# The last V in the buffer of the last K but one, and the MLP's weights behind it

## The chip, the cores and the metric

The kernel runs on one core of a Trainium2 chip. A core has five engines, each with an instruction stream of its own: TensorE (PE in the profile; its weight loads are shown as PEld), VectorE (DVE), ScalarE (ACT), GpSimd (POOL) and SyncE (SP), which here only issues transfers. They wait for each other through semaphores. Each engine works its stream strictly in order, so an instruction that waits holds back all that is behind it. The metric is the device time of one execution in microseconds (us), the median over several runs.

## What is computed

One decoding step of a parallel block: attention over a cache, and beside it an MLP, both added to the input. There are 8 batches, 32 heads with a K and a V of their own each (no sharing), 4096 cached keys, 128 elements a head, a model width D of 640, and 1728 hidden units in the MLP. All tensors are bf16.

```python
def _A_ref(x, k_cache, v_cache, wq, wo):
    q = (x @ wq).reshape(B, 1, 32, 128).transpose(0, 2, 1, 3)
    scores = einsum("bhqd,bhkd->bhqk", q, k_cache) * 128 ** -0.5
    p = softmax(scores)
    o = einsum("bhqk,bhkd->bhqd", p, v_cache)
    return o.transpose(0, 2, 1, 3).reshape(B, 1, 4096) @ wo

def _B_ref(x, w1, b1, w2, b2):
    h = gelu(layernorm(x) @ w1 + b1)
    return h @ w2 + b2

xn = layernorm(x)
return x + _A_ref(xn, k_cache, v_cache, wq, wo) + _B_ref(xn, w1, b1, w2, b2)
```

The two caches hold 256 MiB each and are read once. Everything else together is some 15 MB.

## The kernel before

**Turns.** The work on the caches is cut into NQ = 32 turns; turn i takes one batch and HS = 8 heads. For each turn one K tile and one V tile are loaded whole: 128 partitions with 256 keys of 128 elements each, 64 KB on a partition, 8 MB in all. A partition holds 256 consecutive keys of one head; 16 partitions make a head.

**Buffers.** `S_sb` holds three such slots: KA for the K of even turns, KB for the K of odd turns, VS for every V. All else that is large borrows from them. wq lies in VS before the first V comes. The buffers of the MLP (w1, w2, the hidden values, the widened tail of w1, w2's tail `w2b`) and the selection matrices `selW` and `sel` lie in KA, the rows of wo in KB (woW, woL).

**Scores.** Of the 256 keys on a partition, TensorE takes 80: `pe_T` transposes them in groups of 8, ScalarE copies the result out of PSUM (`act_T`), and `pe_QK` multiplies with the query. VectorE takes the other 176 in three chunks (`dve_chunk`): a product with the query spread over the partitions, a fold that adds one half of each row to the other, and a reduce of what is left. The fold is the second TENSOR_TENSOR of a chunk in the profile. `dve_sel` brings TensorE's scores beside VectorE's, `dve_max` finds the maxima, and `act_exp` computes the exps of 8 heads, with their row sums.

**Product with V.** `pe_RS` adds up the row sums over the partitions and `pe_PV` multiplies the probabilities with V, 256 matmuls in one accumulation. Both of turn i stand in TensorE's stream behind the scores of turn i + 1. `act_O` (ScalarE) copies the result out and `o_norm` (GpSimd; in the last turn VectorE) divides by the sums.

**Behind the turns.** The result has heads and batches in an order that the product with wo can't use, so it is sorted by products with selection matrices: `pe_selw` and `pe_sel` on TensorE, `dve_foldw` and `dve_fold` on VectorE. `fin_wl` and `fin_wn` multiply with wo, whose rows come in six transfers (`load_wl`, `load_wn`), the last ones small. The MLP is `pe_mlp1`, `act_gelu` and `pe_mlp2`; `widen` on GpSimd copies the tail of w1 into a wider layout for it. All of this adds to one sum in PSUM, `ACC_ps`; `fin_store` copies it out and stores it in two halves.

**The order of the work** is written out by hand. `at(position, function)` files each step under a number, Q = 100 for a turn; the steps are sorted by it and called, and each appends its instructions to the list of its engine. Waits are set from the tickets of the steps (`tk`), and a wait that an earlier one of the same engine covers is left out. Then `_replay` writes each list out. For TensorE, VectorE and ScalarE the turns are written as a loop: `_steps` looks for the instructions whose waits grow from turn to turn, and they take their number from the loop's register.

**SyncE's queue** carries all large transfers, in the order of the stream: K i before V i. A K waits until the K before it in its slot has been used (`kt`, `km`, later `exp`), a V until the product with the last V is done (`pv`). The MLP's weights (`load_mlp`, `load_w2b`) wait for the end of K 30's use in KA, so they stand between V 30 and V 31. V 31 waits for the product with V 30, as every V does for the one before. wo waits for the end of K 31's use in KB. V 30 is loaded in two parts (V_CUT: 192 and 64 of the 256 keys), the second with a semaphore of its own (`ld_vl`), for which TensorE waits inside its 256 matmuls. So that the same wait can stand in every turn, the semaphore is raised by 1 at the beginning, by a memset of `consts_pool`, and the number waited for is 1 before turn 30 and 17 from then on.

**TensorE's loop** has 32 turns. The first half of a turn (spread query and scores) is skipped in the last one, by a branch, the second half (sums and product with V) is done in all 32. Behind it stand two stretches under a branch of their own which are done only in turn 31: the MLP's first layer, and the sorting of what is finished by then with the MLP's second layer (`pe_mlp2` at position NQ·Q + 4.6). So in time the MLP's layers come ahead of the sums and product of the last turn. What is left, the product with wo and the sorting of the last turn's result (`pe_sel(3, 1)`), is straight code behind the loop.

The branches of the loop, cut to what decides:

```python
with e.If_lt(reg, n):
    ...                                 # first half
for call in second[0]: ...              # second half
for part in (first[-1][:cut - head[-1]], first[-1][cut - head[-1]:]):
    with e.If_eq(reg, n - 1):
        _replay(e, part)                # MLP; sorting and second layer
```

Of the kernel before, what the change touches and what calls it, by code (L numbers as in the profile page):

```python
# [14 lines left out]
P = 128  # L15
# [100 lines left out]
def _replay(e, calls):  # L116
    for call in calls:
        _emit(e, call)
# [43 lines left out]

def _replay_pe(e, calls, head, mid, end, cut, late):

    n = len(head)
    first = [calls[a:b] for a, b in zip(head, mid)]
    second = [calls[a:b] for a, b in zip(mid, head[1:] + [end])]
    g1, g2 = _steps(first[:-1]), _steps([[c for c in t if not _late(c, late)] for t in second])
    _replay(e, calls[:head[0]])
    with e.bass.Fori(1, n + 1, engines=OrderedEngineSet([e.engine])) as r:  # L170
        reg = e.to_reg(r)
        with e.If_lt(reg, n):
            for call, step in zip(first[0], g1):
                _emit(e, call, call[1][1] + (r - 1) * step if step else None, r)
        g = iter(g2)
        for call in second[0]:
            if _late(call, late):
                e.wait_ge(call[1][0], (r + 1 >> (n.bit_length() - 1)) * 16 + 1)
            else:
                step = next(g)  # L180
                _emit(e, call, call[1][1] + (r - 1) * step if step else None)
        for part in (first[-1][:cut - head[-1]], first[-1][cut - head[-1]:]):
            with e.If_eq(reg, n - 1):
                _replay(e, part)
    assert n & (n - 1) == 0
    _replay(e, calls[end:])


def _late(call, late):
    return call[0] == "wait_ge" and any(call[1][0] is x for x in late)  # L190


def bass_parallel_sum__gqa_block_cached__mixer_channel_mlp__decode_kernel(
# [13 lines left out]
    B, _, D = A_x.shape  # L207
# [31 lines left out]
    WN_CUT = (0, 5 * CT, 7 * CT, 7 * CT + CT // 2, HS * CT)  # L239
    V_CUT = (0, 192, 256)  # L240

# [18 lines left out]
    with ExitStack() as es:  # L260
# [19 lines left out]
        w2_sb = scratch(FB * D, P, KA).rearrange("p (c n) -> p c n", n=D)  # L280
        hT_sb = scratch((FB + FS) * B, P, KA).rearrange("p (c b) -> p c b", b=B)
        b1_sb = scratch(F, 1, KA)
        w1x_sb = scratch(DC * FS * FR, P, KA).rearrange("p (c s n) -> p c s n", c=DC, s=FS)
        b1x_sb = scratch(FS * FR, 1, KA).rearrange("p (c s n) -> p c s n", c=1, s=FS)
        w2b_sb = scratch(FS * D, FR, KA).rearrange("p (s n) -> p s n", s=FS)
        selW_sb = scratch(HW * P, P, KA).rearrange("p (c h r) -> p c h r", c=HW, h=HW)
        sel_sb = scratch(HS * P, P, KA).rearrange("p (c h r) -> p c h r", c=HS, h=HS)
        out_sb = scratch(D, B, KA)
        woW_sb = part(KB, 0, HW * D)
# [61 lines left out]
            _Dma(sem(n)) for n in ("ld_x", "ld_b1", "ld_b2", "ld_wq", "ld_w1", "ld_w2a", "ld_w2b", "st_a", "st_o"))  # L351
        ld_vl = [_Dma(sem(f"ld_vl{q}")) for q in range(1, len(V_CUT) - 1)]
        ld_wl = [_Dma(sem(f"ld_wl{q}")) for q in range(2)]
# [4 lines left out]
        def at(pos, fn, *a):  # L358
            prog.append((pos, len(prog), fn, a))
# [8 lines left out]
        def load_k(i):  # L368
# [7 lines left out]
            tk[("k", i)] = ld_s[s].sig(sp.dma_start(tile[s], cache_src(A_k_cache, i)))  # L376

        def load_mlp():
            sp.wait(tk[("kt", NQ - 2)], tk[("km", NQ - 2)])
            load("w1", ld_w1, w1_sb, B_w1.rearrange("(p c) f -> p c f", c=DC))  # L380
            load("w2a", ld_w2a, w2_sb, B_w2[0:FB * P, :].rearrange("(p c) n -> p c n", c=FB))

        def load_v(i):
            sp.wait(tk["qmm"] if i == 0 else tk[("pv", i - 1)])
            if i != NQ - 2:
                tk[("v", i)] = [ld_s[VS].sig(sp.dma_start(tile[VS], cache_src(A_v_cache, i)))]
                return
            tk[("v", i)] = []
            for d, lo, hi in zip([ld_s[VS]] + ld_vl, V_CUT[:-1], V_CUT[1:]):
                if lo:  # L390
                    d.n += 1
                tk[("v", i)].append(
                    d.sig(sp.dma_start(tile[VS][:, lo:hi, :], cache_src(A_v_cache, i)[:, lo:hi, :])))
# [31 lines left out]
        def consts_pool():  # L425
            pool.iota(iota_h, [[-HP, HS]], base=0, channel_multiplier=1)
            pool.iota(iota_w, [[-RW, HW]], base=0, channel_multiplier=1)
            tk["iota"] = pool.sig(pool.iota(iota_i, [[1, P]], base=0, channel_multiplier=-1))
            for d, (ap, v) in zip([None] + ld_vl + [None] * 2, (
                    (zeros_sb, 0.0), (ones_sb[:, :], 1.0), (mx_sb[:, :], 0.0), (mb_sb[:, :], 0.0))):  # L430
                inst = pool.memset(ap, v)
                if d is not None:
                    inst.call[3] = (d.sem, 1)
# [411 lines left out]
        at(NQ * Q - 60.1, zero_w2b)  # L845
        at(-800, consts_pool)
        at(-795, idents)
        at(NQ * Q - 60, sel_pool)
        at(-790, norm, 0)
# [71 lines left out]
        head, mid, end, cut, done = [], [], [], [], []  # L921

        def mark(to):
            to.append(len(pe.calls))
            pe.waited = {}

        for i in range(1, NQ + 1):
            at(i * Q - 12, mark, head)
            at(i * Q + 47, mark, mid)
        at(NQ * Q + 79, mark, end)  # L930
        at(NQ * Q - 11.2, lambda: cut.append(len(pe.calls)))

# [9 lines left out]
        _replay(nc.gpsimd, pool.calls)  # L942
        _replay_pe(nc.tensor, pe.calls, head, mid, end[0], cut[0], [d.sem for d in ld_vl])
        with nc.allow_low_precision(reason="each sum to bf16 has one bf16 term that is not masked to zero"):
# [32 lines left out]
```

## Time and profile before

| | |
|---|---|
| median of 3 runs | 1281.39 us (1281.37 to 1281.52) |
| profiled execution | 1281.24 us |
| its span, first to last instruction | 1279.9 us |
| bytes moved | 551.97 MB, 431 GB/s over the span |
| busy: TensorE, VectorE, ScalarE, GpSimd | 53%, 86%, 37%, 9% |
| TensorE's granted clock, mean | 0.553 |

The page gives one execution. Its second part cuts the span into 40 slices and shows for each engine the busy share in tenths; below stand the granted clock and the busy share of the DMA engines. The third part lists the DMA queues: q1 is the one that SyncE feeds, q10 ScalarE's, q8 and q14 carry instructions. The timeline has one row for a run of like instructions: start, busy time (both in us), engine, line, operation, what it writes and reads, how often, and in brackets how long the engine had been idle before and what ended that, as far as the semaphores tell; "issue" means that nothing the profile shows was waited for. Since every operation is recorded through one helper, all have the line L111; one goes by the names of the tiles. `PV_ps` belongs to the product with V, `ACC_ps` to the sum (MLP's second layer and wo), `CH_ps` to the row sums, `QB_ps` and `S_ps<-oT_sb` to the sorting, `TR_ps<-xT_sb` to the MLP's first layer. In the chain of waits "PE TR_ps L111 x90" at 1243.41 is that layer too. A DMA row in the timeline shows when a transfer was issued, not when it landed.

### The profile page before, as it was taken

What the parts mean: (1) busy time and instruction counts of PE and PEld (TensorE: products, weight loads), DVE (VectorE), ACT (ScalarE), POOL (GpSimd) and SP (SyncE); (2) the same over time, 40 slices, a digit from 0 to 9 for tenths busy, and PEclk for the clock granted to TensorE, in tenths of its full rate; (3) what the DMA queues carried; (4) which work ended last, traced back from release to release, by engine and by line L of the source; (5) the groups of instructions that cost most, each with busy time, mean ns of one, the idle gap of its engine ahead of it and who ended that gap; (6) DMA issues with size and microseconds to landing.
All of it is one profiled execution on the core that took longest, in us unless ns stands there. A gap on an engine that the chain in (4) does not pass through costs nothing.

```text
span 1279.9 us, 34138 instructions
## 1 busy us (share of the span) xinstructions
PE 672.1 (53%) x13794; PEld 570.6 (45%) x13794; DVE 1103.0 (86%) x684; ACT 476.5 (37%) x906; POOL 109.6 (9%) x121
## 2 busy tenths in 40 slices
PE   2536555446645446545456554456454466464476
PEld 0435444435535345444345444345343355353465
DVE  2899998889888889888899888898888898888894
ACT  0524444233444233443234443234443334442331
POOL 0020010000000000000000000000000000000050
PEclk8656655565565556555555555555565556655665
DMA  9999999999999999999999999999999999999998
GB/s 424 425 431 429 434 434 428 440 434 430 432 438 428 438 432 432 434 432 434 430 440 430 432 434 438 428 432 436 430 438 432 432 432 440 426 434 436 426 444 365
DMA packets 10784, 551.97 MB, mean 431 GB/s; under 512 B 1242, under 2 KB 1523, under 8 KB 1812
## 3 DMA queue, kind: packets, MB, share of 16 engines
q1 hardware_dynamic: 10736, 551.79, 99.7%
q8 instruction: 8, 0.13, 0.0%
q14 instruction: 4, 0.03, 0.0%
q10 hardware_dynamic: 36, 0.02, 0.0%
HBM read 551.80 MB, written 0.01 MB: 431 GB/s over the span
## 4 chain that ended last, share of the span: by engine, by line
DMA 46%; DVE 37%; issue 12%; ACT 4%; PE 1%; DVEq 0%; SPq 0%
DMA S_sb<-in_A_k_cache_dram 42%; DVE S_sb L111 26%; DVE Sd_sb L111 8%; ACT P_sb L111 4%; DMA S_sb<-in_B_w_dram 2%; DMA S_sb<-in_A_wo_dram 2%; DVE S_ps L111 1%; PE TR_ps L111 1%; DVE mx_sb L111 1%; DVE mxT_sb L111 0%; DVE mbT_sb L111 0%; DVEq L109 0%; DVE mq_sb L111 0%; DVE NB_sb L111 0%; DVE ri_sb L111 0%
## 5 line engine op out<-in xcount | busy, mean ns | idle before, releaser
L111 PE MATMUL TR_ps<-ident_bf,S_sb 128*128 128x128 bf16 (+1 forms) x2578 | 341.8, 279 | 354.1 <-POOL kr_sb L111 331.4
L111 DVE TENSOR_TENSOR S_sb<-S_sb,qbc_sb 128x7552 bf16<-128x7552 bf16 (+1 forms) x96 | 388.8, 4050 | 127.2 <-DMA S_sb<-in_A_k_cache_dram 126.9
L111 PEld LDWEIGHTS TR_ps<-ident_bf,S_sb 128*128 (+2 forms) x2578 | 245.1, 103 | 412.4 <-issue 339.6
L111 DVE TENSOR_REDUCE Sd_sb<-S_sb 128x59 f32<-128x3776 bf16 (+1 forms) x96 | 390.2, 4065 | 6.0
L111 ACT ACTIVATE KT_sb<-TR_ps 128x1024 bf16<-128x1024 bf16 x320 | 326.6, 1023 | 120.5 <-PE TR_ps L111 109.4
L111 PE MATMUL PV_ps<-P_sb,S_sb 128*128 128x8 bf16 x8192 | 224.0, 175 | 141.3 <-DMA S_sb<-in_A_v_cache_dram 138.3
L111 PEld LDWEIGHTS PV_ps<-P_sb,S_sb 128*128 128x128 bf16 x8192 | 221.4, 103 | 144.1 <-DMA S_sb<-in_A_v_cache_dram 141.0
L111 DVE TENSOR_TENSOR S_sb<-S_sb 128x3776 bf16<-128x3776 bf16 (+1 forms) x96 | 206.5, 2151 | 3.3
L111 ACT ACTIVATE P_sb<-Sd_sb,NB_sb 128x256 bf16<-128x256 f32 x256 | 126.3, 494 | 210.1 <-DVE NB_sb L111 210.1
L111 PE MATMUL S_ps<-qrep_sb,KT_sb 128*128 128x8 bf16 x2560 | 121.9, 177 | 50.3 <-ACT KT_sb L111 47.0
L111 ACT ACTIVATE oU_sb<-PV_ps 128x8 f32<-128x8 f32 x31 | 5.5, 177 | 377.5 <-PE PV_ps L111 377.5
L111 PEld LDWEIGHTS S_ps<-qrep_sb,KT_sb 128*128 128x128 bf16 x2560 | 91.8, 103 | 82.2 <-ACT KT_sb L111 40.0
L111 POOL TENSOR_TENSOR oT_sb<-oU_sb,ri_sb 128x8 bf16<-128x8 f32 x31 | 71.5, 2306 | 371.4 <-DVE S_sb L111 315.3
L111 POOL COPY qrep_sb<-qT_sb 128x128 bf16<-128x128 bf16 x32 | 18.5, 578 | 470.0 <-PE S_ps L111 453.3
L111 ACT ACTIVATION_READ_ACCUMULATOR P_sb<-Sd_sb,NB_sb 128x1 f32 x256 | 47.7, 186 | 0.0
L111 DVE TENSOR_TENSOR S_ps<-S_ps,mask_sb 128x320 f32<-128x320 f32 (+1 forms) x65 | 31.6, 486 | 2.7 <-PE S_ps L111 2.7
L111 DVE TENSOR_REDUCE Sd_sb<-S_ps 128x40 f32<-128x320 f32 x64 | 31.5, 492 | 2.2
L111 ACT ACTIVATE qbc_sb<-QB_ps 128x128 bf16<-128x128 f32 x32 | 8.9, 277 | 58.2 <-PE QB_ps L111 58.2
L111 PE MATMUL QB_ps<-ident_bf,qrep_sb 128*128 128x128 bf16 x32 | 9.1, 283 | 40.2 <-DVE S_sb L111 21.9
L111 POOL MEMSET kr_sb<- 128x1 f32 x32 | 3.1, 98 | 295.2 <-DMA S_sb<-in_A_k_cache_dram 295.2
L111 PEld LDWEIGHTS QB_ps<-ident_bf,qrep_sb 128*128 128x128 bf16 x32 | 3.3, 103 | 43.1 <-ACT oU_sb L111 29.1
L111 PE MATMUL CH_ps<-rs_sb,ones_f 128*128 128x8 f32 x64 | 16.2, 326 | 6.1 <-ACT P_sb L111 6.1
(70 smaller groups left out, 150.1 us busy)
## 6 DMA issues: line engine op xcount, KB each, us to landing
S_sb<-in_A_v_cache_dram SPq DMA_DIRECT2D x1, 6144.0 KB, 26.8
S_sb<-in_A_wq_dram SPq DMA_DIRECT2D x1, 5120.0 KB, 15.2
S_sb<-in_A_wo_dram SPq DMA_DIRECT2D x1, 2560.0 KB, 18.4
S_sb<-in_B_w_dram SPq DMA_DIRECT2D x1, 2160.0 KB, 30.3
S_sb<-in_B_w_dram SPq DMA_DIRECT2D x1, 2080.0 KB, 34.8
S_sb<-in_A_v_cache_dram SPq DMA_DIRECT2D x1, 2048.0 KB, 31.3
S_sb<-in_A_wo_dram SPq DMA_DIRECT2D x1, 1280.0 KB, 21.1
S_sb<-in_A_wo_dram SPq DMA_DIRECT2D x1, 800.0 KB, 22.6
```

The costliest lines, as they stand in the source:

```text
L111: inst = getattr(e, name)(*a, **k)
```

## The change

V 31 goes to KA, the buffer of K 30, and no longer waits for the product with V 30: it is issued as soon as K 30 is used up (`kt`, `km` of turn 30), right behind V 30. V 30 is loaded whole, as one transfer, and the semaphore `ld_vl`, its waits and its raising by a memset go. The MLP's buffers and the selection matrices move from KA to VS. What fills them now waits for the product with V 30: w1 and w2 on SyncE, b1 on ScalarE, the zeros of `w2b` and the two copies of `sel_pool` on GpSimd. The order of the large transfers becomes V 30, V 31, w1 and w2, wo.

TensorE's loop becomes a plain one of 31 turns without branches; what the last turn had under a branch, and its sums and product with V, become straight code behind it. There the order changes as well: sorting of what is finished, sums and product of turn 31, the MLP's first layer, the sorting of the last turn, the MLP's second layer, wo.

```diff
-def _replay_pe(e, calls, head, mid, end, cut, late):
+def _replay_pe(e, calls, head):
+    turns = [calls[a:b] for a, b in zip(head, head[1:])]
+    grow = _steps(turns)
     _replay(e, calls[:head[0]])
...
+    with e.bass.Fori(1, len(turns) + 1, engines=OrderedEngineSet([e.engine])) as r:
+        for call, step in zip(turns[0], grow):
+            _emit(e, call, call[1][1] + (r - 1) * step if step else None, r)
+    _replay(e, calls[head[-1]:])
...
-    V_CUT = (0, 192, 256)
...
-        o_ = {KA: 0, KB: 0}
+        o_ = {VS: 0, KB: 0}
...
-        w1_sb = scratch(DC * F, P, KA).rearrange("p (c n) -> p c n", c=DC)
+        w1_sb = scratch(DC * F, P, VS).rearrange("p (c n) -> p c n", c=DC)
...
+        def vslot(i):
+            return KA if i == NQ - 1 else VS
+
         def load_mlp():
-            sp.wait(tk[("kt", NQ - 2)], tk[("km", NQ - 2)])
+            sp.wait(tk[("pv", NQ - 2)])
...
         def load_v(i):
-            sp.wait(tk["qmm"] if i == 0 else tk[("pv", i - 1)])
-            if i != NQ - 2:
-                tk[("v", i)] = [ld_s[VS].sig(sp.dma_start(tile[VS], cache_src(A_v_cache, i)))]
-                return
...
+            s = vslot(i)
+            if i == NQ - 1:
+                sp.wait(tk[("kt", NQ - 2)], tk[("km", NQ - 2)])
+            else:
+                sp.wait(tk["qmm"] if i == 0 else tk[("pv", i - 1)])
+            tk[("v", i)] = ld_s[s].sig(sp.dma_start(tile[s], cache_src(A_v_cache, i)))
...
         def load_b1():
-            act.wait(tk[("kt", NQ - 2)], tk[("km", NQ - 2)])
+            act.wait(tk[("pv", NQ - 2)])
...
         def zero_w2b():
-            pool.wait(tk[("kt", NQ - 2)], tk[("km", NQ - 2)])
+            pool.wait(tk[("pv", NQ - 2)])
...
         def sel_pool():
-            pool.wait(tk["id"], tk[("kt", NQ - 2)], tk[("km", NQ - 2)])
+            pool.wait(tk["id"], tk[("pv", NQ - 2)])
...
         def pe_PV(i):
             PVB.use(pe)
             pe.wait(tk[("exp", i)])
+            pe.wait(tk[("v", i)])
             for j in range(NKEY):
-                if j == 0:
-                    pe.wait(tk[("v", i)][0])
-                elif j in V_CUT:
-                    pe.wait_ge(ld_vl[V_CUT.index(j) - 1].sem, 1)
-                last = pe.matmul(PV_ps[:, 0:HS], tile[VS][:, j, :], P_sb[:, :, j],
+                last = pe.matmul(PV_ps[:, 0:HS], tile[vslot(i)][:, j, :], P_sb[:, :, j],
                                  start=(j == 0), stop=(j == NKEY - 1))
...
-        at(NQ * Q - 55, load_mlp)
-        at(NQ * Q - 54.9, load_w2b)
+        at(NQ * Q + 40, load_mlp)
+        at(NQ * Q + 40.1, load_w2b)
...
-        at(NQ * Q - 11.7, widen)
-        at(NQ * Q - 11.5, pe_mlp1)
-        at(NQ * Q - 11, act_gelu)
-        at(NQ * Q + 4.6, pe_mlp2)
+        at(NQ * Q + 50.5, widen)
+        at(NQ * Q + 50.6, pe_mlp1)
+        at(NQ * Q + 50.7, act_gelu)
+        at(NQ * Q + 79.05, pe_mlp2)
...
-            at(o + 50, load_v, i)
+            at(o + 50 if not last else o + 49.9, load_v, i)
...
-        at(o + 79.2, pe_sel, 3, 1)
-        at(o + 79.5, dve_fold, 3, 1)
+        at(o + 79.02, pe_sel, 3, 1)
+        at(o + 79.03, dve_fold, 3, 1)
```

More of the change, by code (lines that the diff above doesn't have):

```diff
@@ L160, in _replay_loop @@
     _replay(e, calls[b:])
-def _replay_pe(e, calls, head, mid, end, cut, late):
[L165 to L168, printed above, removed]
-    _replay(e, calls[:head[0]])
[L170 to L190, printed above, removed]
+def _replay_pe(e, calls, head):
+    turns = [calls[a:b] for a, b in zip(head, head[1:])]
+    grow = _steps(turns)
+    _replay(e, calls[:head[0]])
+    with e.bass.Fori(1, len(turns) + 1, engines=OrderedEngineSet([e.engine])) as r:
+        for call, step in zip(turns[0], grow):
+            _emit(e, call, call[1][1] + (r - 1) * step if step else None, r)
+    _replay(e, calls[head[-1]:])
 def bass_parallel_sum__gqa_block_cached__mixer_channel_mlp__decode_kernel(
@@ L278, in bass_parallel_sum__gqa_block_cached__mixer_channel_mlp__decode_kernel @@
         wq_sb = part(VS, 0, DC * H * DH).rearrange("p (c n) -> p c n", c=DC)
-        w1_sb = scratch(DC * F, P, KA).rearrange("p (c n) -> p c n", c=DC)
[L280 to L288, printed above, removed]
+        w1_sb = scratch(DC * F, P, VS).rearrange("p (c n) -> p c n", c=DC)
+        w2_sb = scratch(FB * D, P, VS).rearrange("p (c n) -> p c n", n=D)
+        hT_sb = scratch((FB + FS) * B, P, VS).rearrange("p (c b) -> p c b", b=B)
+        b1_sb = scratch(F, 1, VS)
+        w1x_sb = scratch(DC * FS * FR, P, VS).rearrange("p (c s n) -> p c s n", c=DC, s=FS)
+        b1x_sb = scratch(FS * FR, 1, VS).rearrange("p (c s n) -> p c s n", c=1, s=FS)
+        w2b_sb = scratch(FS * D, FR, VS).rearrange("p (s n) -> p s n", s=FS)
+        selW_sb = scratch(HW * P, P, VS).rearrange("p (c h r) -> p c h r", c=HW, h=HW)
+        sel_sb = scratch(HS * P, P, VS).rearrange("p (c h r) -> p c h r", c=HS, h=HS)
+        out_sb = scratch(D, B, VS)
         woW_sb = part(KB, 0, HW * D)
@@ L351, in bass_parallel_sum__gqa_block_cached__mixer_channel_mlp__decode_kernel @@
             _Dma(sem(n)) for n in ("ld_x", "ld_b1", "ld_b2", "ld_wq", "ld_w1", "ld_w2a", "ld_w2b", "st_a", "st_o"))
-        ld_vl = [_Dma(sem(f"ld_vl{q}")) for q in range(1, len(V_CUT) - 1)]
         ld_wl = [_Dma(sem(f"ld_wl{q}")) for q in range(2)]
@@ L428, in consts_pool @@
             tk["iota"] = pool.sig(pool.iota(iota_i, [[1, P]], base=0, channel_multiplier=-1))
[L429 to L433, printed above, removed]
+            for ap, v in ((zeros_sb, 0.0), (ones_sb[:, :], 1.0), (mx_sb[:, :], 0.0), (mb_sb[:, :], 0.0)):
+                pool.memset(ap, v)
             tk["consts"] = pool.sig(pool.memset(ones_f[:, :], 1.0))
         def sel_pool():
-            pool.wait(tk["id"], tk[("kt", NQ - 2)], tk[("km", NQ - 2)])
+            pool.wait(tk["id"], tk[("pv", NQ - 2)])
             tk["selw"] = pool.sig(pool.tensor_copy(
@@ L920, in bass_parallel_sum__gqa_block_cached__mixer_channel_mlp__decode_kernel, with mark @@
                 at((LOOP0 + 2 * m) * Q - 12, lambda n=n: marks[n].append(len(engs[n].calls)))
-        head, mid, end, cut, done = [], [], [], [], []
-        def mark(to):
-            to.append(len(pe.calls))
+        head, done = [], []
+        def mark():
+            head.append(len(pe.calls))
             pe.waited = {}
         for i in range(1, NQ + 1):
[L928 to L931, printed above, removed]
+            at(i * Q - 12, mark)
         for _, _, fn, a in sorted(prog, key=lambda t: (t[0], t[1])):
@@ L942, in bass_parallel_sum__gqa_block_cached__mixer_channel_mlp__decode_kernel @@
         _replay(nc.gpsimd, pool.calls)
-        _replay_pe(nc.tensor, pe.calls, head, mid, end[0], cut[0], [d.sem for d in ld_vl])
+        _replay_pe(nc.tensor, pe.calls, head)
         with nc.allow_low_precision(reason="each sum to bf16 has one bf16 term that is not masked to zero"):
```

10 lines of the change are left out of this document (2 added, 8 removed).

## The prediction

> **What bounds the kernel now.** I read the page first: its 40 slices, then the queues. All times are microseconds from the start of the span.
>
> ```profile
> span 1279.9 us, 34138 instructions
> ...
> DMA  9999999999999999999999999999999999999998
> ...
> q8 instruction: 8, 0.13, 0.0%
> ```
>
> The DMA row is the bound: 9 or more tenths in all but the last slice. The change moves no byte more or less, so it can only matter through what runs behind the last bytes. That is the end of the chain of waits:
>
> ```profile
> 1243.41 7.93 PE TR_ps L111 x90
> ...
> 1277.38 0.04 issue
> 1277.43 0.48 PE ACC_ps L111 x10
> ...
> 1278.27 0.32 DVE S_sb L111
> ```
>
> The last rows of wo land at 1277.38, ten matmuls and a copy later the output leaves at 1278.27: only some 2.5 us lie behind the stream. To see what the stream does I took SyncE's issues from the timeline, then TensorE's work at the end:
>
> ```profile
> 1139.11 0.33 SPq L111 DMA_DIRECT2D S_sb<-in_A_k_cache_dram  x1
> ...
> 1177.81 0.33 SPq L111 DMA_DIRECT2D S_sb<-in_A_k_cache_dram  x1
> ...
> 1210.85 12.52 SPq L111 DMA_DIRECT2D S_sb<-in_B_w_dram  x10
> 1238.17 0.34 SPq L111 DMA_DIRECT2D S_sb<-in_A_v_cache_dram  x1
> 1253.16 2.71 SPq L111 DMA_DIRECT2D S_sb<-in_A_wo_dram  x6
> ```
>
> ```profile
> 1253.09 2.27 PE L111 MATMUL ACC_ps<-S_sb 128*8 128x160 bf16 x60
> ...
> 1256.16 0.61 PE L111 MATMUL QB_ps<-oT_sb,S_sb 128*128 128x56 bf16 x8 [0.26 <-DVE oS_sb L111]
> ...
> 1265.47 7.00 PE L111 MATMUL PV_ps<-P_sb,S_sb 128*128 128x8 bf16 x256 [5.93 <-DMA S_sb<-in_A_v_cache_dram]
> 1272.72 2.30 PE L111 MATMUL ACC_ps<-S_sb,oW_sb 128*8 128x160 bf16 x64 [0.26 <-DVE oT_sb L111]
> 1274.96 0.38 PE L111 MATMUL S_ps<-oT_sb,S_sb 128*128 128x8 bf16 x8
> 1275.27 1.90 PE L111 MATMUL ACC_ps<-S_sb,oS_sb 128*8 128x160 bf16 x52
> 1277.43 0.65 PE L111 MATMUL ACC_ps<-S_sb,oS_sb 128*8 128x160 bf16 x12 [0.26 <-DMA S_sb<-in_A_wo_dram]
> ```
>
> K 30 and K 31 are issued 38.70 apart: one K and one V take 38.7, one of them 19.35. K 31 lands at 1216.6 (the first row of GpSimd below starts behind it). Behind it stand V 30, the MLP's weights, V 31 and wo. V 31 lands at 1265.4 (its PV starts at 1265.47), 48.8 after K 31, so w1 and w2 take 48.8 - 38.7 = 10.1. PV of turn 31 takes 7.0, the product with wo 2.3 + 0.4 + 1.9 + 0.65, partly paced by its landings. TensorE has the MLP behind it by then: its first layer, the 7.93 from 1243.41, lies under V 31, and so does its second, the 2.27 from 1253.09.
>
> **The order of the transfers.** After the change V 31 is issued where w1 was, 1210.85, behind V 30: V 30 lands whole at 1216.6 + 19.35 = 1235.95, V 31 at 1255.3. w1 and w2 need the buffer of V 30, so PV 30: 1236.0 + 7.0 = 1243.0. They are issued at 1243.1, 12 before the queue runs dry, and take their 10.1 behind V 31: w1 to about 1260.4, w2 to 1265.4. The SyncE issues cost 12.52 for the ten DMAs even with a wait for GpSimd inside: done by 1255.7 at the latest. wo stands behind them on SyncE and was issued at 1253.16; it has until 1265.4. So wo lands at 1277.4 as before, and the stream gains and loses nothing: 0. V 30 as one DMA instead of two, its whole wait instead of two waits (its PV ends at 1243.0 instead of 1238.1, where SyncE goes on today; what waits for it on ScalarE and GpSimd is counted below), the memsets without a signal, the branches that go from TensorE's loop: 0, because the turns are paced by the transfers.
>
> **What the moved waits do to GpSimd and VectorE.**
>
> ```profile
> 1216.68 4.03 DVE L111 TENSOR_TENSOR S_sb<-S_sb,qbc_sb 128x7424 bf16<-128x7424 bf16 x1 [4.26 <-DMA S_sb<-in_A_k_cache_dram]
> 1220.74 5.67 DVE L111 TENSOR_TENSOR S_sb<-S_sb 128x3712 bf16<-128x3712 bf16 x1
> ...
> 1242.72 4.04 DVE L111 TENSOR_TENSOR S_sb<-S_sb,qbc_sb 128x7552 bf16<-128x7552 bf16 x1
> 1246.80 2.16 DVE L111 TENSOR_TENSOR S_sb<-S_sb 128x3776 bf16<-128x3776 bf16 x1
> ...
> 1254.68 0.70 DVE L111 TENSOR_TENSOR QB_ps<-QB_ps,mask_sb 128x512 f32<-128x512 f32 x1
> ```
>
> ```profile
> 1216.65 1.16 POOL L111 MEMSET S_sb<- 48x1280 bf16 x1
> 1217.76 10.56 POOL L111 COPY S_sb<-ident_bf 128x2048 bf16<-128x2048 bf16 x2
> ...
> 1246.77 3.43 POOL L111 COPY S_sb<-S_sb 1x32 bf16<-1x32 bf16 x8
> ```
>
> Today the copies that make selW and sel stand at 1217.76, beside chunk 0 of K 31. The first waits for the product (ends 1220.71) and runs 3.6; the fold behind it takes 5.67 instead of the 2.16 of its like at 1246.80, so VectorE loses 3.5; the second copy waits for that fold (1226.41) and runs 1.9, to 1228.32. After the change they wait for PV 30. VectorE gets its 3.5 back at 1220.74: chunk 2 starts at 1239.2, its fold at 1243.2, its reduce ends at 1249.6 (today 1253.1, where SyncE goes on), and the exps can start at 1251.2 (today 1254.76, below). GpSimd starts at 1243.05 with its memset (1.16), so its copy comes at 1244.2, behind the start of the fold, and waits until that ends at 1245.35. Then 3.6 + 1.9: selW at 1249.0, sel at 1250.9, o_norm of turn 30 by 1251.5. The other way round, the fold waits for the copy and the 3.5 are lost again. [...]
>
> ```profile
> 1238.31 0.24 ACTq L111 DMA_DIRECT2D S_sb<-in_B_b_dram  x1
> ...
> 1251.38 0.32 ACT L111 ACTIVATE S_sb<-TR_ps 128x104 bf16<-128x104 f32 x2 [11.51 <-PE TR_ps L111]
> ...
> 1254.76 0.51 ACT L111 ACTIVATE P_sb<-Sd_sb,NB_sb 128x256 bf16<-128x256 f32 x1 [1.77 <-DVE NB_sb L111]
> ...
> 1258.61 0.19 ACT L111 ACTIVATION_READ_ACCUMULATOR P_sb<-Sd_sb,NB_sb 128x1 f32 x1
> ```
>
> The eight exps take 4.05, so those of turn 31 end at 1255.2. On TensorE stand in order: the sel products, the row sums, PV 31, then (moved) the MLP's first layer, and behind it sel of the last turn, the second layer and wo. sel's second part waits for a fold of VectorE, 1.4 as between 1254.68 and 1256.16: sel at 1251.0 to 1251.7, the fold to 1253.1, the part of group 3 from 1253.2 to 1253.8. The row sums go at 1255.4 and PV 31 at 1255.8, 9.7 earlier than now. If nothing stops it, it ends at 1262.8. Then everything else is in series: first layer 7.93, gelu 0.4 (0.32 from 1251.38 and the handing over), second layer 2.27, wo 2.3 + 1.9 + 0.65, together 15.45 (sel of the last turn hides in the gelu): 1278.25. TensorE ends today at 1277.43 + 0.65 = 1278.1. So the order alone costs 0.2. V 31's transfer no longer covers the MLP; w2 and wo cover it just so, and each us that PV 31 ends later than 1262.8 is one more at the end. b1, issued at 1243.3, needs at most the 5.1 from 1238.31 to 1243.41 and isn't late; widening w1 on GpSimd (3.43) ends by 1264, before the first layer needs it.
>
> **TensorE's code.** This is the term that I take as deciding. PV 31 stood in the loop and was run from code that was there; after the change the loop has only 31 turns, and PV 31, sel, MLP and wo are straight code behind it, run once. What new code costs under a full queue shows in the first turn:
>
> ```profile
> 74.84 4.47 PE L111 MATMUL PV_ps<-P_sb,S_sb 128*128 128x8 bf16 x161 [0.44 <-DMA S_sb<-in_A_v_cache_dram]
> 82.30 2.68 PE L111 MATMUL PV_ps<-P_sb,S_sb 128*128 128x8 bf16 x95 [2.99 <-issue]
> 97.89 0.29 PE L111 MATMUL QB_ps<-ident_bf,qrep_sb 128*128 128x128 bf16 x1 [12.91 <-issue]
> ...
> 120.47 6.97 PE L111 MATMUL PV_ps<-P_sb,S_sb 128*128 128x8 bf16 x256
> ```
>
> ```profile
> q8 instruction: 4, 0.07, 1.0%
> ```
>
> ```profile
> 0.00:47.40 47.40, 16.52 (x223) 11.01 (x224) 18.82 (x30) 11.85 (x15) 1.93 (x16) 0.82 0.99 420
> ...
> 97.80:128.20 30.40, 20.25 (x419) 17.15 (x419) 29.79 (x20) 14.49 (x28) 0.75 (x2) 0.61 0.99 427
> 1204.70:1256.70 52.00, 33.16 (x601) 28.64 (x601) 46.89 (x31) 19.54 (x40) 21.00 (x14) 0.57 1.00 429
> 1256.70:1280.00 23.30, 12.64 (x396) 11.20 (x394) 7.16 (x16) 2.69 (x12) 0.00 (x0) 0.57 0.84 353
> ```
>
> The first PV stops after 161 pairs for 2.99 that no wait explains ("issue"), the next turn starts after another 12.91; from the second turn on (120.47) the same 256 pairs go through in 6.97. In that stretch q8 fetches instructions four times, 16 KB each. Different code is 224 pairs ahead of the loop, 419 of a turn, 601 - 419 of the MLP's turn and, less PV 31 and its row sums, 394 - 258 behind: 961 pairs, or 1922 instructions and some control; q8 brings eight blocks for it (page), so a block is about 250 instructions, 125 pairs. From the block before, entered 125 pairs ahead of the stop (at about 75.8), to the resumption at 82.30 are 6.5; the two blocks behind it take (97.89 - 82.30) / 2 = 7.8 each. So one block is fetched ahead, when the one before is entered, and takes 6.5 to 7.8 under K and V. Towards 20 KB descriptors I expect less: b1's 5.1 above is the nearest row, and I take 6.3 there. Bounds: 5.1 and 7.8.
>
> Where the blocks end after the change: the block that began at pair 161 of the first PV holds 95 pairs and then the loop's end, 190 instructions; the remaining 60 are the straight code's first, which is sel (32 pairs, 64 instructions). The next block, fetched already in the first turn, is thus entered with the end of sel, at 1253.5, and holds 125 pairs of PV 31: to 1255.8 + 3.4 = 1259.2. The block behind it comes at 1253.5 + 7.1 = 1260.6: stop 1.4. It holds the rest of PV 31 but for some pairs, 3.5: 1264.1. The next one was asked for at 1260.6 and comes at 1266.9: stop 2.8, before the last pairs or the first layer. The first layer takes 7.93 for one block and hides the next fetch; the last one, asked for in the second layer at about 1276.4, is needed at about 1281; the transfers are through at 1277.4, so 0 to 1, and I take 0.2. Sum: 0.2 + 1.4 + 2.8 + 0.2 = **4.6**. With 5.1 per block, stops of 0 and 1.6: 1.8 in all. With 7.8: 2.1 and 4.3, and 1 at the end: 7.6.
>
> [...]
>
> The profiled execution took 1281.24 with a span of 1279.9; the median is 1281.39, 0.15 above it. Span 1279.9 + 4.6 = 1284.5, against the median 1286.0.
>
> **The rivals.** A: the code is there in time, because the descriptors of w1 and w2 are shorter, or because the fetch is asked for earlier than I think (at the wait of sel). Against: the first turn. Then the 0.2 of the order is left: 1281.6, not slower by what can be measured. It decides if PV 31 ends before 1265.0 (2.2 behind 1262.8: with the 0.2 and the 0.2 above, the end has moved by 2.6). B: GpSimd's copy gets ahead of the fold. VectorE has no 3.5 to spare, the exps end at 1258.7, PV 31 starts at 1259.3, stops 1.1 and 2.8 come on top: 1281.39 + 3.5 + 4.3 = 1289.2. For it: 1 us between the two starts; against: the order of the two today. C: faster. The stream has no byte less and 2.5 behind it; I find no mechanism beyond some tenths. D: the stops are longer, if a block is entered only behind the exps (1255.2): 1.7 more, 1287.7; inside the forecast's range.
>
> **How the numbers follow.** A measurement of this kernel tells 0.2%, 2.6 us, from no change. Forecast with D (stops of 2.4 to 7.6): 0.60. A: 0.22. B or a later PV for another reason: 0.16. C: 0.02. Slower 0.76, same 0.22, faster 0.02. The time is the forecast's, 1286.0; the range reaches from A's 1281.6 to a little above B, 1290.0, and leaves some 0.1 out.
>
> **What would show it.** In the profile after: V 31 landing at 1255.3 and wo at 1277.4 (the stream); the fold of chunk 0 at 2.1 instead of 5.67; PV 31 starting at 1255.8 and broken by an idle put down to "issue" after some 125 pairs, a second one at its end, with q8 fetching three or four times between 1250 and 1285; the first layer from about 1267; the matmuls of wo in series behind it without waiting for DMA. A PV 31 in one piece of 7 us would make me wrong on the code; one that starts at 1259 wrong on GpSimd; a gap in the DMA row before 1277 wrong on the stream.

## The result and the profile after

The changed kernel takes 1292.33 us (median of 6 runs, 1291.15 to 1293.03), the kernel before 1281.36 beside it: a ratio of 1.0084, 95% interval 1.0074 to 1.0094. Forecast were 1286.0, and 1281.6 to 1290.0. So it is slower, as forecast, but by 11.0 instead of 4.6. The profiled execution took 1292.26 with a span of 1291.0.

First the page of the changed kernel, with SyncE's issues from its timeline (start, busy time, engine, what it writes and reads, how often):

```profile
span 1291.0 us, 33941 instructions
...
DMA  9999999999999999999999999999999999999995
...
q8 instruction: 10, 0.16, 0.0%
```

```profile
1177.84 0.33 SPq L111 DMA_DIRECT2D S_sb<-in_A_k_cache_dram  x1
1204.33 6.90 SPq L111 DMA_DIRECT2D S_sb<-in_A_v_cache_dram  x2
1243.03 6.74 SPq L111 DMA_DIRECT2D S_sb<-in_B_w_dram  x10
1256.12 2.72 SPq L111 DMA_DIRECT2D S_sb<-in_A_wo_dram  x6
```

K 31 goes out at 1177.84 (before: 1177.81), so nothing has happened up to here. The DMA engines are only half busy in the last slice of the span, and q8 brought ten packets of code (0.16 MB, 16 KB each), two more than before. V 30 and V 31 stand together, w1 and w2 at 1243.03, wo at 1256.12. The DMA view of the stretch from 1240 to 1291, in 40 slices of 1.275, shows where the stream ends:

```profile
DMA  8979999897499999999989989999800000000000
GB/s 360 514 308 514 411 463 465 360 514 308 196 420 434 434 427 418 418 418 424 515 350 450 442 361 418 416 393 388 284 23 0 0 0 0 13 0 0 13 0 8
```

The last slice in which the stream runs, the one with 284 GB/s, ends at 1240 + 29 x 1.275 = 1277.0. By the transfers' semaphores in the traces V 31 landed at 1255.33 (forecast 1255.3) and the last piece of wo at 1278.02, against 1277.80 before: the stream has lost 0.2. What is new is some 11 us behind it, until the output is issued at 1289.31, without a large transfer. VectorE and GpSimd around PV 30's end, and ScalarE's first exp:

```profile
1220.78 2.09 DVE L111 TENSOR_TENSOR S_sb<-S_sb 128x3712 bf16<-128x3712 bf16 x1
...
1239.19 4.04 DVE L111 TENSOR_TENSOR S_sb<-S_sb,qbc_sb 128x7552 bf16<-128x7552 bf16 x1
1243.26 8.66 DVE L111 TENSOR_TENSOR S_sb<-S_sb 128x3776 bf16<-128x3776 bf16 x1
1251.95 4.09 DVE L111 TENSOR_REDUCE Sd_sb<-S_sb 128x59 f32<-128x3776 bf16 x1
```

```profile
1243.07 1.16 POOL L111 MEMSET S_sb<- 48x1280 bf16 x1 [26.31 <-PE PV_ps L111]
1244.17 5.76 POOL L111 COPY S_sb<-ident_bf 128x2048 bf16<-128x2048 bf16 x2
```

```profile
1257.73 0.51 ACT L111 ACTIVATE P_sb<-Sd_sb,NB_sb 128x256 bf16<-128x256 f32 x1 [14.51 <-DVE NB_sb L111]
```

The fold of chunk 0 fell from 5.67 to 2.09 as forecast, and chunk 2 starts 3.5 earlier. But its fold, the row at 1243.26, takes 8.66 where 2.1 was forecast: it ends at 1251.92, 2.0 after the second of GpSimd's two copies (1244.17 + 5.76). The exps start at 1257.73; forecast were 1251.2, before it was 1254.76. TensorE from the row sums on (in the first layer's place stands its row of the chain of waits):

```profile
1261.82 0.59 PE L111 MATMUL CH_ps<-rs_sb,ones_f 128*128 128x8 f32 x2 [2.02 <-ACT P_sb L111]
1262.26 3.51 PE L111 MATMUL PV_ps<-P_sb,S_sb 128*128 128x8 bf16 x126
1268.48 3.56 PE L111 MATMUL PV_ps<-P_sb,S_sb 128*128 128x8 bf16 x128 [2.71 <-issue]
1274.69 0.20 PE L111 MATMUL PV_ps<-P_sb,S_sb 128*128 128x8 bf16 x2 [2.65 <-issue]
...
1283.19 2.27 PE L111 MATMUL ACC_ps<-S_sb 128*8 128x160 bf16 x60
1285.39 2.31 PE L111 MATMUL ACC_ps<-S_sb,oW_sb 128*8 128x160 bf16 x64
1287.48 1.45 PE L111 MATMUL ACC_ps<-S_sb,oS_sb 128*8 128x160 bf16 x64
```

```profile
1274.89 7.91 PE TR_ps L111 x90
```

PV 31 starts 6.46 later than forecast (1262.26 for 1255.8) and stops twice, 2.71 and 2.65, without a wait that the profile can name. Behind it all is in series; wo no longer waits for DMA. The account of TensorE's end: forecast without stops 1278.25; + 6.46 for the late start; + 5.36 for the stops; + 0.27 for PV 31's three pieces (12.63 from start to end, less 7.0 and 5.36); - 1.41, since from PV 31's end on the series takes 14.04 (1274.89 to 1288.93) and not 15.45, wo being there whole. Sum 1288.93, which is the end of the last row.

### The profile page after: what moved, and what is told of

It reads as the page before. It is cut to its first block, busy times and chain, and to the rows that moved or that the text cites. A ratio compares the mean times of both kernels' runs of the same rounds, so it can differ in the third digit from the quotient of the medians.

```text
span 1291.0 us, 33941 instructions
## 1 busy us (share of the span) xinstructions
PE 670.4 (52%) x13794; PEld 568.3 (44%) x13794; DVE 1105.9 (86%) x684; ACT 475.6 (37%) x905; POOL 102.1 (8%) x121
## 4 chain that ended last, share of the span: by engine, by line
DMA 45%; DVE 37%; issue 12%; ACT 4%; PE 2%; DVEq 0%; SPq 0%
DMA S_sb<-in_A_k_cache_dram 45%; DVE S_sb L111 26%; DVE Sd_sb L111 7%; ACT P_sb L111 4%; DVE S_ps L111 1%; PE TR_ps L111 1%; DVE mx_sb L111 1%; PE PV_ps L111 1%; PE ACC_ps L111 0%; DVE mbT_sb L111 0%; DVE mxT_sb L111 0%; DVE NB_sb L111 0%; DVE mq_sb L111 0%; DVE ri_sb L111 0%; DVE mb_sb L111 0%
## 5 line engine op out<-in xcount | busy, mean ns | idle before, releaser
L111 DVE TENSOR_TENSOR S_sb<-S_sb 128x3776 bf16<-128x3776 bf16 (+1 forms) x96 | 209.4, 2182 | 3.3
L111 PEld LDWEIGHTS CH_ps<-rs_sb,ones_f 128*128 128x128 f32 x64 | 12.8, 250 | 6.2 <-DVE S_sb L111 4.1
L111 DVE TENSOR_REDUCE mx_sb<-Sd_sb 128x1 f32<-128x256 f32 x32 | 13.4, 420 | 1.1
```

Source lines behind the costliest of these rows:

```text
L111: inst = getattr(e, name)(*a, **k)
```

## The experiments

Two theories were open for the 8.66: GpSimd's copies hold the fold, or something else in that stretch does (V 31's transfer, the new buffers). And two for the stops: code that comes late, or a wait of another kind. Each diff is against the changed kernel unless it says otherwise. Medians stand against 1281.3 to 1281.4 for the kernel before.

**The fold first.** All of GpSimd's work of this stretch waits for the fold of chunk 2.

```diff
         def zero_w2b():
-            pool.wait(tk[("pv", NQ - 2)])
+            pool.wait(tk[("pv", NQ - 2)], tk[("fold", NQ - 1)])
...
             t = dve.sig(dve.tensor_tensor(kt[:, :, 0:DH // 2], kt[:, :, 0:DH // 2], kt[:, :, DH // 2:DH], ALU.add))
+            tk[("fold", i)] = t
```

> The changed kernel, but GpSimd's memset and copies for selW and sel wait for VectorE's fold of K 31's chunk 2 as well. Theory P (GpSimd's memset at 1243.07 comes just ahead of the fold and holds it off for 6.5): the fold takes 2.1 instead of 8.66, the exps start at 1251.2 instead of 1257.73, PV 31 at 1255.8, and the end moves 6.5 earlier: 1285.8. The two stops in PV 31 stay, about 2.7 each. Rival Q (what costs is only the work in series behind V 31 on TensorE, whose start is set by something else): PV 31 starts no earlier than 1260 and the time stays within 2 of 1292.3.

Measured: 1287.6, ratio 1.0047 [1.0030, 1.0064]. VectorE, GpSimd and TensorE of this run:

```profile
1243.34 2.12 DVE L111 TENSOR_TENSOR S_sb<-S_sb 128x3776 bf16<-128x3776 bf16 x1
...
1250.54 1.97 DVE L111 TENSOR_SCALAR mb_sb<-mq_sb 128x32 f32<-128x32 f32 x1
```

```profile
1246.69 5.78 POOL L111 COPY S_sb<-ident_bf 128x2048 bf16<-128x2048 bf16 x2
```

```profile
1257.59 3.52 PE L111 MATMUL PV_ps<-P_sb,S_sb 128*128 128x8 bf16 x126
1263.09 3.57 PE L111 MATMUL PV_ps<-P_sb,S_sb 128*128 128x8 bf16 x128 [1.99 <-issue]
1269.85 0.20 PE L111 MATMUL PV_ps<-P_sb,S_sb 128*128 128x8 bf16 x2 [3.18 <-issue]
```

The fold is back at 2.12, so it was GpSimd that held it. That is worth 4.7 of the 11.0, less than the 6.5: a small operation on the scores' maxima (`mb_sb`, 0.18 before) now takes 1.97 and ends with the second copy (1246.69 + 5.78 = 1252.47). The large reduce ahead of it (1245.49, 4.09), though beside the copies too, was not slowed. The two stops stay, at 1.99 and 3.18.

**Which of GpSimd's operations.** First, only the copies wait for the fold, and the memset stays ahead of it; then only the second copy waits. The ticket `fold` is set as in the first experiment.

```diff
         def sel_pool():
-            pool.wait(tk["id"], tk[("pv", NQ - 2)])
+            pool.wait(tk["id"], tk[("pv", NQ - 2)], tk[("fold", NQ - 1)])
```

> The changed kernel with GpSimd's memset where it is, ahead of VectorE's fold, but the two copies waiting for that fold. [...] If it was only the copies queued behind the memset: the fold takes 2.1. If GpSimd's memset makes the fold lose its turn for good, it can't here, since the copies wait for it. In either case the exps start at 1253 to 1254, and the time is 1287 to 1289.

```diff
                 selW_sb[:, :, :, :],
                 ident_bf[:, :].rearrange("p (r c) -> p c r", c=HW)[:, :, None, :].to_broadcast([P, HW, HW, RW])))
+            pool.wait(tk[("fold", NQ - 1)])
             tk["sel"] = pool.sig(pool.tensor_copy(
                 sel_sb[:, :, :, :],
```

> The changed kernel where only the second of GpSimd's two copies waits for the fold of chunk 2; the memset and the first copy stay as they are. Theory, that a copy queued right behind the memset gets ahead of a fold that is ready: the fold holds what is left of the memset and the first copy, 1.0 + 3.8, ahead of its own 2.1, so 6.7 to 6.9 us in the row, and the time is some 1.8 under the changed kernel's, about 1290.5. Rival, that only the second copy stops the fold: the fold takes 2.1 and the time is about 1286.

Measured in one execution each: 1285.73 and 1290.3. VectorE and GpSimd with both copies held back:

```profile
1243.30 2.13 DVE L111 TENSOR_TENSOR S_sb<-S_sb 128x3776 bf16<-128x3776 bf16 x1
...
1250.50 0.82 DVE L111 TENSOR_SCALAR mb_sb<-mq_sb 128x32 f32<-128x32 f32 x1
```

```profile
1243.14 1.16 POOL L111 MEMSET S_sb<- 48x1280 bf16 x1 [26.34 <-PE PV_ps L111]
1245.49 5.79 POOL L111 COPY S_sb<-ident_bf 128x2048 bf16<-128x2048 bf16 x2 [1.20 <-DVE S_sb L111]
```

and with the second held back:

```profile
1243.63 6.73 DVE L111 TENSOR_TENSOR S_sb<-S_sb 128x3776 bf16<-128x3776 bf16 x1
```

```profile
1244.54 3.83 POOL L111 COPY S_sb<-ident_bf 128x2048 bf16<-128x2048 bf16 x1
1250.42 1.99 POOL L111 COPY S_sb<-ident_bf 128x1024 bf16<-128x1024 bf16 x1 [2.05 <-DVE S_sb L111]
```

The memset alone does not hold a fold that runs beside it (2.13). The run with both copies held back came out below its expectation of 1287 to 1289: `mb_sb` was held only for 0.82, to the end of the second copy (1251.28), and the exps started at 1251.87 and not at 1253 to 1254. With one copy behind the memset the fold takes 6.73, ending 2.0 after that copy (1248.37): it runs behind it, although by its row it had started 0.9 before the copy did. So of the changed kernel's 8.66, 2.1 are the fold itself, 4.6 come with the first copy and 1.93 with the second.

**The copies ahead of the memset.**

```diff
-        at(NQ * Q - 30.1, zero_w2b)
+        at(NQ * Q - 29.9, zero_w2b)
```

> The changed kernel with GpSimd's memset behind the two copies instead of ahead of them. If each engine's next operation takes its turn, as in the kernel before (fold 5.67 between the two copies): the first copy waits for VectorE's product and runs 3.8, then the fold, 5.9 in all, then the second copy; exps at 1254.9, end 2.8 earlier: 1289.5. [...]

Measured: 1288.83, ratio 1.0058 [1.0041, 1.0075].

```profile
1243.45 5.65 DVE L111 TENSOR_TENSOR S_sb<-S_sb 128x3776 bf16<-128x3776 bf16 x1
```

```profile
1243.26 7.69 POOL L111 COPY S_sb<-ident_bf 128x2048 bf16<-128x2048 bf16 x2 [26.32 <-PE PV_ps L111]
```

Now they take turns, as in the kernel before (5.67 there): copy, fold, copy, since the two copies together last 7.69, the fold's 2 longer than 5.8. So the fold lost its turn to the second copy with the memset ahead of the copies, and kept it without. Why, these runs don't show.

**The copies on ScalarE.** ScalarE is idle from 1243.2 on.

```diff
-        def sel_pool():
-            pool.wait(tk["id"], tk[("pv", NQ - 2)])
-            tk["selw"] = pool.sig(pool.tensor_copy(
+        def sel_act():
+            act.wait(tk["id"], tk[("pv", NQ - 2)])
+            tk["selw"] = act.sig(act.activation(
...
-        at(NQ * Q - 30, sel_pool)
+        at(NQ * Q - 11.75, sel_act)
```

> The changed kernel with the two copies that make selW and sel on ScalarE, which is idle there, instead of GpSimd; the memset stays. [...]

Measured: 1284.44, ratio 1.0023 [1.0013, 1.0032]. ScalarE and TensorE:

```profile
1243.58 5.86 ACT L111 ACTIVATE S_sb<-ident_bf 128x2048 bf16<-128x2048 bf16 x2 [0.24 <-issue]
1251.30 0.51 ACT L111 ACTIVATE P_sb<-Sd_sb,NB_sb 128x256 bf16<-128x256 f32 x1 [1.87 <-DVE NB_sb L111]
```

```profile
1255.84 6.92 PE L111 MATMUL PV_ps<-P_sb,S_sb 128*128 128x8 bf16 x254
1265.20 0.20 PE L111 MATMUL PV_ps<-P_sb,S_sb 128*128 128x8 bf16 x2 [2.44 <-issue]
...
1279.63 0.85 PE L111 MATMUL ACC_ps<-S_sb,oS_sb 128*8 128x160 bf16 x33 [1.02 <-issue]
```

ScalarE needs the same time for the two copies (5.86) and holds nothing: fold 2.12, `mb_sb` 0.18, exps at 1251.30 and PV 31 at 1255.84, which are the forecast's own places, 1251.2 and 1255.8. So all of the 6.46 came from the copies on GpSimd. This run fell below the 1285.9 to 1286.9 expected of it, since only one of the two stops in PV 31 is left; the other one is gone for a reason that is open (below). One of 1.02 has come in the product with wo. And the time is 2.0 to 2.4 longer than the span in eight of this run's ten executions, 1.3 to 1.4 in the other two and in the changed kernel: some 0.9 lie behind the last instruction that the profile counts. The tenth packet of q8 stands there, at 1283.88, behind the span's end of 1282.5; that it is what this time waits for is not shown.

**The code moved by 64 instructions.** 32 tiny matmuls ahead of the loop, whose result nobody reads, move all later code against the blocks in which it is fetched (q8's packets of 16 KB). Each matmul is two instructions, a weight load and the matmul (13794 of each on the page of the changed kernel): a pair.

```diff
             acc(ident_bf[0:B, 0:B], x_sb)
             acc(ones_sb[:, :], b2_sb)
+            for _ in range(32):
+                pe.matmul(CH_ps[0:B, 0:B], zeros_sb[:, 0:B], zeros_sb[:, 0:B], start=True, stop=True)
```

> The changed kernel with 32 small matmuls more (64 instructions, two a matmul) far ahead of the loop, where TensorE waits for wq. They change no result; they move all later code by 64 instructions. Theory C (the stops in PV 31 are code that is fetched late, at fixed distances in the code): the first block end falls 32 pairs earlier, after 94 pairs, and its block is asked for while TensorE waits for PV 30 and sel, so it is there and doesn't stop; the second falls after 222 pairs instead of 254 and stops 2.7. One stop less: 1289.6. Rival D (the stops come from data, the clock or the transfers at that time): both stay at 126 and 254 pairs, 1292.3.

Measured: 1288.35, ratio 1.0054 [1.0038, 1.0071].

```profile
1262.16 6.07 PE L111 MATMUL PV_ps<-P_sb,S_sb 128*128 128x8 bf16 x222
1270.25 1.06 PE L111 MATMUL PV_ps<-P_sb,S_sb 128*128 128x8 bf16 x34 [2.02 <-issue]
```

Nothing of what PV 31 works on has changed, and yet its stops are at other places: after 222 pairs instead of 126 and 254, that is 32 pairs earlier than 254, and the one that would stand at 94 does not occur: the packet of q8 ahead of PV 31 came at 1246.84, while TensorE still waited for the sorting. A wait for data would not move with the code. And a packet of q8 lands in each stop of PV 31, in all the runs (here at 1268.79, in the stop from 1268.23 to 1270.25). The stops are code. That the time fell by 4.0, more than expected, is for 3.3 the stop of 2.02 in the place of 5.36; the rest are tenths, in PV 31's start, its fewer pieces and wo.

**The code moved by 8 instructions.** The same with four matmuls, against the changed kernel.

```diff
+            for _ in range(4):
+                pe.matmul(CH_ps[0:B, 0:B], zeros_sb[:, 0:B], zeros_sb[:, 0:B], start=True, stop=True)
```

> The changed kernel with four tiny matmuls more (eight instructions) among PV 31's predecessors. Theory, that a code block is asked for when the one before it is entered: the block's end moves back by eight instructions, to a place ahead of the row sums' wait for the exponentials, so the next block is entered at about 1259.8 instead of 1261.8; PV 31 stops after some 122 pairs, its first stop shrinks from 2.7 to about 0.7 us, the second stays at 2.65; time about 1290.3. Rival, that a stop lasts as long wherever the block is entered: the first stop stays at about 2.7 and the time at 1292.3.

Measured: 1291.96, ratio 1.0084 [1.0067, 1.0101], hardly different from the changed kernel (1291.15 to 1293.03).

```profile
1262.17 3.40 PE L111 MATMUL PV_ps<-P_sb,S_sb 128*128 128x8 bf16 x122
1267.62 3.56 PE L111 MATMUL PV_ps<-P_sb,S_sb 128*128 128x8 bf16 x128 [2.04 <-issue]
1273.55 0.32 PE L111 MATMUL PV_ps<-P_sb,S_sb 128*128 128x8 bf16 x6 [2.36 <-issue]
```

The places are right to the pair (122, 250), the size is not: the first stop fell by 0.67 and not by 2.0. The packets of q8 in the trace show where the time goes:

```
                 block entered     fetch starts  landed    TensorE goes on
changed kernel   1261.82           1265.97       1267.02   1268.48
changed kernel   1268.48           1272.33       1273.39   1274.69
changed kernel   1274.69           1275.90       1277.33   (needed later)
changed kernel   about 1284.2      1284.38       1285.34   (needed later)
8 instructions   about 1259.4      1265.29       1266.34   1267.62
8 instructions   1267.62           1271.15       1272.21   1273.55
ScalarE copies   about 1259.3      1262.73       1263.77   1265.20
ScalarE copies   1279.63           1283.88       1285.08   (behind the span)
```

An entry with "about" is counted out in pairs from the last stop. A fetch that TensorE stood still for took 1.0 to 1.1 itself, and TensorE went on 1.3 to 1.5 after it had landed. The rest, 3.5 to 4.2 in the rows where the entry is seen and the stream runs, is the time from entering a block to the start of the next one's packet. Near the end of the stream it is 1.2, and behind it, at 1284.2, it is 0.2. So most of a stop would fit a packet that stands in line behind the stream's, though no row shows the line itself. Three places don't fit that alone. In this run 5.9 lie between the place where I put the entry and the packet. With the copies on ScalarE the first block's packet started at 1256.58, only 1.2 behind the row sums (1255.39), so it had been asked for earlier. And the last packet of that run came 4.25 after the entry although the stream was over. What exactly asks for a block, above all while TensorE waits, is open.

**Both, with either remedy for the fold.** The fold first together with the 32 matmuls, and the copies on ScalarE together with them.

> Both edits. If P and C are right and independent, 6.5 + 2.7 come off: 1283.1. If they share their gain (a stop that is hidden only by the later start), 1285.8.

> The last one with the 32 small matmuls ahead of the loop as well. Only one stop of 2 to 2.5 is left in PV 31, behind 222 pairs: 3 to 4 less than the run without them, 1282 to 1283. Then wo's transfers are nearly the bound again, and the rest of the gain is lost to waits for their landings. If the order of the change could beat the kernel before, this run would have to come below 1281.4; I expect it not to.

Measured: 1284.38, ratio 1.0023 [1.0014, 1.0033], and 1283.31, ratio 1.0016 [1.0007, 1.0026]. TensorE of the second:

```profile
1255.67 6.07 PE L111 MATMUL PV_ps<-P_sb,S_sb 128*128 128x8 bf16 x222
1263.80 1.06 PE L111 MATMUL PV_ps<-P_sb,S_sb 128*128 128x8 bf16 x34 [2.05 <-issue]
...
1278.29 0.23 PE L111 MATMUL ACC_ps<-S_sb,oW_sb 128*8 128x160 bf16 x1 [0.74 <-issue]
```

The first came out between its two cases (1283.1 and 1285.8), the second above its 1282 to 1283. In the first `mb_sb` is still held, and its PV 31 starts at 1257.53, 1.9 later than in the second. The second gained 1.1 on the run without the small matmuls, and not the 3 to 4 expected, since that run had lost one stop already. It is the best version of the change, 9.0 below it and still 1.9 above the kernel before. The two stops left in it, 2.05 and 0.74, are more than that. But wo's last piece landed at 1279.03 in its trace, two of its sixteen parts 1.2 later than the others (1277.82), and that alone would keep TensorE from ending where it did before (1278.08). What held these parts is not shown; the code's packets, 1.1 each, may have. So whether the order alone, with the code in time, would cost nothing is open and was not run.

**The kernel before with straight code.** The slots and the order of before, but V 30 whole, a plain loop of 31 turns and the rest straight. Against the kernel before:

```diff
-    V_CUT = (0, 192, 256)
+    V_CUT = (0, 256)
...
-def _replay_pe(e, calls, head, mid, end, cut, late):
+def _replay_pe(e, calls, head):
...
+    _replay(e, calls[head[-1]:])
```

> The kernel before with the code part of the change alone: TensorE's plain loop of 31 turns, the last turn's work straight behind it in the order of before (MLP, sorting, second layer, then PV 31), V 30 as one transfer. Transfers, buffers and GpSimd stay as before. Theory C (straight code is fetched one block ahead and a block takes 6 to 7 under full transfers, so PV 31's 256 fast pairs outrun it): the blocks that are entered while PV 31 waits for its V are there, the one behind is not; one stop of 2 to 3.5 in PV 31, which now ends with nothing to hide it: 1283.5 to 1285. Rival (the fetching costs only where TensorE is late for another reason, or is hidden by the wait for V 31): 1281.4.

Measured: 1284.74, ratio 1.0026 [1.0016, 1.0036].

```profile
1250.65 0.44 PE L111 MATMUL TR_ps<-xT_sb,S_sb 128*128 128x8 bf16 x5 [7.69 <-issue]
...
1266.47 6.35 PE L111 MATMUL PV_ps<-P_sb,S_sb 128*128 128x8 bf16 x232 [1.74 <-DMA S_sb<-in_A_v_cache_dram]
1274.65 0.79 PE L111 MATMUL PV_ps<-P_sb,S_sb 128*128 128x8 bf16 x24 [1.82 <-issue]
...
1279.78 1.24 PE L111 MATMUL ACC_ps<-S_sb,oS_sb 128*8 128x160 bf16 x32 [0.63 <-issue]
```

```profile
1250.68 1.54 POOL L111 COPY S_sb<-S_sb 1x32 bf16<-1x32 bf16 x8 [3.83 <-DMA S_sb<-in_B_b_dram]
```

The 7.69 at 1250.65 looks like code and is none: no packet of q8 lies in that stretch, and GpSimd's row of the same moment names what both waited for, the small transfer of b1, issued at 1243.13 and landed at 1250.56. It costs little, since V 31 is not there before. PV 31 starts 1.0 later than before (1265.47): V 31, issued at 1242.99 behind the whole V 30 instead of 1238.17, lands that much later, and this part of it is not straight code. The two stops behind it, 1.82 and 0.63, are. 1.0 + 1.82 + 0.63 is 3.45, and 3.35 were measured, but the two are not the same thing: TensorE ends only 2.9 later than before (1281.02 for 1278.08), since it no longer waits for wo, and 0.8 of the time lie behind the span, as in the run with the copies on ScalarE (time less span is 1.9 to 2.5 in all ten executions, for 1.3; q8's tenth packet at 1284.41, span's end 1283.05). So the stops of the straight tail are some 2.4 here, and that the time fell into the range expected for one stop of 2 to 3.5 is in part luck.

## Why the prediction was right or wrong

- **The order of the transfers, 0**: right to 0.2. V 31 landed at 1255.33 (1255.3), wo's last piece at 1278.02 for 1277.80 before. b1 took 8.2 (1243.18 to 1251.37) where "at most the 5.1" was said; it was in time all the same.
- **VectorE gets 3.5 back**: right. Fold of chunk 0 2.09, chunk 2 at 1239.19 (1239.2).
- **"GpSimd starts at 1243.05 with its memset (1.16), so its copy comes at 1244.2, behind the start of the fold, and waits until that ends at 1245.35"**: the step that failed. The times are right to 0.1, the order is not: the fold, started at 1243.26, was held until both copies were through. Price 6.46 at the start of PV 31, where the forecast had 0. By the rows the fold began 0.9 before the first copy and ended behind both. That the copy would wait for a fold begun ahead of it was an estimate from the kernel before (a fold of 5.67 between the two copies), and no run shows it for the copy behind the memset: with the memset ahead the fold took 8.66, and 6.73 with one copy. Rival B had the mechanism, at 3.5, since it let the fold go between the copies as in the kernel before; the run with the copies ahead of the memset is where that happened (5.65).
- **Even with the fold first the exps would have been late**: the prediction had no term for the second copy holding `mb_sb` (1.97 for 0.18).
- **The code, stops of 1.4 and 2.8**: that late code stops PV 31 is right, a packet of q8 landing in each stop (1267.02 and 1273.39); the terms were mis-sized: 2.71 and 2.65. The two stops stand 128 pairs apart (behind 126 and 254), so a block is 128 pairs, 256 instructions, rather than 125 pairs, and a block begins with the two row sums, which wait for the exps. So in the changed kernel that block is entered behind the exps, as in rival D (1.7 more; 1.3 more at the first stop). From entry to resumption 6.66 and 6.21 passed, where 7.1 and 6.3 had been taken. Each of PV 31's stops took 1.8 to 3.2 over all the runs; in five of the eleven with straight code one of its two block ends went without a stop.
- **The series behind PV 31, 15.45**: 14.04, as wo is no longer paced by its landings. The 0.2 taken for a last stop did not come in the changed kernel.
- **The direction**: slower was forecast, for the code. The code's stops did cost more than forecast, but the larger part of the 11.0 came from the step that failed. Less the 6.46 the account would give 1285.9, next to the forecast's 1286.0; that nearness is luck, since it is made of stops that are 1.2 longer and a series that is 1.4 shorter.
- **The range**: it stopped a little above B with the forecast's stops. B at its true size together with D lay outside.

## What to carry to other kernels

Work that is moved off the end of a transfer stream must be checked for the engines that it now runs beside: here two copies that had cost 3.5 in a place with slack cost 6.5 on the critical chain, and handing them to an idle ScalarE took all of that away. Code that runs once behind a loop was fetched here while the data's transfers ran (packets of q8 at 1265.97 and 1272.33, the stream's end at 1277): 128 pairs of weight load and matmul ran in 3.5, and where it stood still for a block, TensorE went on 5.9 to 6.7 after entering the one before. So look where the ends of the blocks fall (here 128 pairs apart), above all behind a wait. And an idle that the profile puts down to "issue" was code in some rows here (2.71) and a semaphore in another (7.69, for b1): the place of the stop when the code is shifted, or a neighbour waiting for the same thing, tells which.

## What the runs showed of the hardware that was not expected

- A VectorE fold that by its row had started 0.9 before a GpSimd copy ended only after that copy when a memset of GpSimd ran at that moment (8.66 with two copies, 6.73 with one), while with the copies directly behind the product they took turns (5.65), and the memset alone did nothing (2.13).
- A TENSOR_SCALAR of 128x32 was held by the same copies (1.97 for 0.18), while reduces and transposes beside them kept their times (4.09, 0.21).
- Copies of the same size took 5.86 on ScalarE and 5.8 on GpSimd, and on ScalarE held neither the fold (2.12) nor `mb_sb` (0.18).
- A fetch of 16 KB that TensorE stood still for took 1.0 to 1.1, but under the stream it started only 3.5 to 4.2 after the block before had been entered, in the three stops for which that entry is seen, and TensorE went on only 1.3 to 1.5 after the landing.
